# One u tile moved from TensorE to the crossbar, adds of u in another order, and transposes ahead of an output store

## The chip, the cores and the metric

The kernel runs on one core of a Trainium2 chip. The metric is the device time of one execution in microseconds (us), the median over runs. TensorE is PE in the profile, its weight loads PEld, VectorE DVE, ScalarE ACT, GpSimd POOL, SyncE SP.

## The reference

Eight batches of causal attention over a window of 64 positions, then a mixer of low rank along the sequence, then a two layer MLP.

```python
def reference(q, k, v, U, V, w1, w2):        # q, k, v: (8, 8, 576, 64)
    scores = where(0 <= i - j < 64, q @ k.T / 8, -1e9)
    x = concat_heads(softmax(scores) @ v)                # (8, 576, 512)
    u = x + ((x.T @ U) @ V).T                            # rank 32
    return u + relu(u @ w1) @ w2                         # 512 -> 2048 -> 512
```

## The kernel before

The 4608 rows of u are cut into nine chunks of 512 for the MLP. The attention of the next batch is woven into the fills of PE of the current chunk: `slots` lists what follows each fill, and `PLACE` tables give the places. Fills 0 to 15 are the first layer (`ch1`, tile psA), 16 to 31 the second (`ch2`, tile psU, four quarters for each of four row tiles). A batch has 576 rows, four and a half tiles of 128, so chunks and batches do not line up.

The parts that the change touches:

```python
def VM(ts, banks=None):              # u = x + low rank part, for tiles ts
    def up():
        if banks is None:
            pair = ps_big.tile([P, 2, CH], FP32, name="psv", tag="big")
            ...
        for n in range(2):
            nc.tensor.matmul(ps[0][n], vrep[half, ...], hh["sb"][half, ...], ...)
    def add(n):
        def f():
            ...
            nc.vector.tensor_tensor(out=u_tiles[g][rs, cs], in0=ps[0][n][rs],
                                    in1=x[...], op=ALU.add)
        return f
    return [up, add(0), add(1)]

def UT(t):                           # u tile -> its transpose, for the first MLP layer
    def f():
        g = g0 + t
        dst = uT_of(g // TPC)[:, g % TPC, :, :]
        if b >= NXT:                 # NXT = 3: crossbar transpose, issued by SyncE
            nc.sync.dma_start_transpose(out=dst, in_=u_tiles[g][:])
            return
        tp = ps_tp.tile([P, NDC, P], BF16, name="tpu", tag="tp")   # a single bank
        for dc in range(NDC):
            nc.tensor.transpose(tp[:, dc, :], u_tiles[g][...], ident[:])
        nc.scalar.copy(out=dst, in_=tp[:])
    return f

def two_banks():                     # for tile 4: one bank of mm, and the tp bank
    return (psum["mm"].tile(..., name="psv0", tag="mm"),
            ps_tp.tile([P, CH], FP32, name="psv1", tag="tp"))

def mixed(parts=None):
    parts = parts or [VM((NT - 1,), two_banks), VM((0, 1)), VM((2, 3))]
    for part in parts:
        part[0]()
    for part in parts:
        for add in part[1:]:
            add()
```

In the profile, un is a tile of u, psv what the six matmuls of the V part write, uTc the transposed u, and tpu the PSUM tile of a PE transpose; it and psv1 share the one bank of the tag tp, the tp bank. A crossbar transpose is done by the DMA (DMA_TRANSPOSE in the profile). Before the V part, `hh["sb"]` (the low rank result) is spread over the partitions by DVE copies:

```python
nc.scalar.copy(out=part[:], in_=hh["ps"][high])
nc.vector.tensor_tensor(out=hh["sb"][low], in0=hh["ps"][low], in1=part[:], op=ALU.add)
nc.vector.tensor_copy(out=hh["sb"][high], in_=hh["sb"][low])
```

The softmax here doesn't subtract the row's maximum and nothing guards it: scores larger than these inputs give would overflow.

## Time and profile before

| | before |
|---|---|
| median of the first three runs (range) | 311.64 us (311.27 to 311.76) |
| profiled span | 310.6 us |
| PE busy | 301.8 us, 97% |
| first psA matmul | 22.66 us |
| PE transposes into tpu / crossbar transposes into uTc | 36 / 23 |

The first psA matmul divides the span in two: a start-up, in which PE waits for the first loads, and what I call the body, from there to the end of the last add into osb (307.85 us, so 285.19 us). In the body PE hardly stops, so its length is close to a sum of PE pieces. It divides into nine chunks, each from its first psA piece to the next one's in the view of the chain.

### The profile page before, as it was taken

The page shows a single profiled execution, that of the slowest core. Times are in us where ns is not written, and L with a number is a line of the kernel's source. Part 1 is how long each engine was busy: PE and PEld are TensorE (multiplying, and loading weights), DVE is VectorE, ACT ScalarE, POOL GpSimd, SP SyncE. Part 2 cuts the span into 40 slices and gives each one's busy share as a digit, 9 for nine tenths or more (in the row PEclk, how much of TensorE's full clock was granted, in tenths as well). Part 3 has the DMA queues.
Part 4 walks back from the last instruction along what each step waited for, and adds up shares of the span by engine and source line. Part 5 has one row for each costly group of instructions (what it writes and reads, how often), then busy time and mean ns, then how long its engine had stood idle before and what let it go on. Part 6 is the DMA issues. An engine that isn't in the chain of part 4 may idle for free.

```text
span 310.6 us, 6952 instructions
## 1 busy us (share of the span) xinstructions
PE 301.8 (97%) x2881; PEld 147.6 (48%) x2903; DVE 175.1 (56%) x336; ACT 108.2 (35%) x173; POOL 102.0 (33%) x136
## 2 busy tenths in 40 slices
PE   7799999999999999999999999999999999999996
PEld 7453554544545544454445444544454444444443
DVE  4485566528667873677557765666566542116011
ACT  3555680358127620543044304440354004101500
POOL 8693264294695091437143705000000000000000
PEclk9999999999999999999999999999999999999999
DMA  7999999999999999999599999932400275011011
GB/s 107 170 209 208 204 172 145 147 148 160 138 148 157 139 142 203 130 156 172 103 150 141 184 118 132 175 103 74 132 2 0 68 222 203 32 69 36 0 65 70
DMA packets 156495, 39.87 MB, mean 128 GB/s; under 512 B 145040, under 2 KB 151440, under 8 KB 156464
## 3 DMA queue, kind: packets, MB, share of 16 engines
q0 software_dynamic: 104720, 18.88, 82.0%
q1 hardware_dynamic: 51744, 20.55, 34.0%
q8 instruction: 22, 0.36, 0.5%
q14 instruction: 9, 0.07, 0.1%
HBM read 37.97 MB, written 9.44 MB: 153 GB/s over the span
## 4 chain that ended last, share of the span: by engine, by line
PE 93%; DMA 3%; issue 1%; DVE 1%; POOL 1%; ACT 0%; POOLq 0%
PE psA L765 41%; PE psU L789 40%; DMA qr<-in_q_dram 3%; PE sc L347 3%; PE xw L409 2%; PE psv L660 2%; PE pshh L533 1%; PE tpu L694 1%; PE tpg L283 1%; PE low L347 0%; PE psh L533 0%; DVE xs L420 0%; POOL kr L120 0%; PE tpw L283 0%; PE xe L409 0%
## 5 line engine op out<-in xcount | busy, mean ns | idle before, releaser
L765 PE MATMUL psA<-uTc,w1b 128*128 128x512 bf16 (+1 forms) x584 | 131.2, 377 | 0.3 <-DVE uTc L635 0.3
L789 PE MATMUL psU<-w2b,c 128*128 128x512 bf16 (+2 forms) x572 | 127.3, 373 | 1.3 <-issue 0.3
L789 PEld LDWEIGHTS <-c 128*128 128x128 bf16 x592 | 56.0, 98 | 66.0 <-issue 2.9
L765 PEld LDWEIGHTS <-w1b 128*128 128x128 bf16 x584 | 54.3, 98 | 63.9 <-issue 2.6
L777 ACT ACTIVATE c<-psA 128x512 bf16<-128x512 f32 x84 | 50.1, 597 | 83.6 <-PE psA L765 83.3
L775 DVE TENSOR_SCALAR c<-psA 128x512 bf16<-128x512 f32 x60 | 41.3, 689 | 40.9 <-PE psA L765 40.9
L802 DVE TENSOR_TENSOR osb<-psU,un 128x512 f32<-128x512 f32 (+2 forms) x29 | 19.5, 671 | 52.4 <-PE psU L789 52.4
L367 ACT ACTIVATE pts<-sc 128x1024 bf16<-128x1024 f32 x32 | 31.3, 1028 | 2.3 <-PE sc L347 2.3
L138 POOL DMA_DIRECT2D vA<-in_v_dram x32 | 28.3, 913 | 7.4 <-DMA w1b<-in_moe_w_ch_dram 2.7
L675 DVE TENSOR_TENSOR un<-psv,xs 128x512 bf16<-128x512 f32 (+3 forms) x48 | 26.1, 593 | 4.3 <-PE psv L660 4.0
L129 POOL DMA_DIRECT2D qr<-in_q_dram x30 | 26.7, 888 | 4.1 <-PE tpg L283 1.7
L129 POOL DMA_DIRECT2D kr<-in_k_dram x30 | 26.6, 887 | 3.4 <-PE sc L347 2.0
L400 ACT ACTIVATE ptl<-low 128x256 bf16<-128x256 f32 x6 | 2.3, 384 | 61.0 <-PE high L347 61.0
L373 DVE TENSOR_TENSOR pts<-pts,maskA 128x1024 bf16<-128x1024 bf16 x28 | 19.1, 682 | 1.7 <-ACT pts L367 1.7
L500 DVE TENSOR_TENSOR xs<-xw,rcw 128x896 bf16<-128x896 f32 x14 | 15.3, 1091 | 0.5
L963 POOL COPY held<-qf 1x1 bf16<-1x1 bf16 x5 | 0.9, 178 | 42.9 <-DMA qf<-qr 42.9
L347 PEld LDWEIGHTS <-kf 64*64 64x64 bf16 x704 | 9.8, 107 | 7.3 <-issue 7.0
L347 PE MATMUL sc<-qf,kf 64*64 64x128 bf16 (+1 forms) x608 | 11.5, 212 | 0.5 <-DVE qf L300 0.3
L409 PEld LDWEIGHTS <-pts 128*64 128x64 bf16 x512 | 9.8, 110 | 3.5 <-issue 2.5
L697 ACT COPY uTc<-tpu 128x512 bf16<-128x512 bf16 x9 | 5.3, 586 | 11.4 <-PE tpu L694 11.4
L409 PE MATMUL xw<-vA,pts 128*64 128x65 bf16 x217 | 8.4, 195 | 0.0
L974 POOL COPY held<-uTc 1x1 bf16<-1x1 bf16 x3 | 0.5, 177 | 23.6 <-DMA uTc<-un 23.6
(125 smaller groups left out, 190.7 us busy)
## 6 DMA issues: line engine op xcount, KB each, us to landing
out_dram<-osb SPq DMA_DIRECT2D x27, 256.0 KB, 2.3
vA<-in_v_dram POOLq DMA_DIRECT2D x32, 128.0 KB, 6.4
kr<-in_k_dram POOLq DMA_DIRECT2D x24, 128.0 KB, 5.4
qr<-in_q_dram POOLq DMA_DIRECT2D x24, 128.0 KB, 5.5
w2b<-in_moe_w_ch_dram POOLq DMA_DIRECT2D x4, 512.0 KB, 15.8
out_dram<-late SPq DMA_DIRECT2D x8, 256.0 KB, 4.2
vB<-in_v_dram POOLq DMA_DIRECT2D x8, 128.0 KB, 8.8
w1b<-in_moe_w_ch_dram POOLq DMA_DIRECT2D x2, 512.0 KB, 11.1
```

The source lines that it names most:

```text
L129: nc.gpsimd.dma_start(out=dst[0:rows, t, :, :], in_=src[b, :, t * P : t * P + rows, :].rearrange("h p d -> p h d"),)
L138: nc.gpsimd.dma_start(out=dst[:, :, 0:D], in_=v[b, :, lo : lo + P, :].rearrange("h p d -> p h d"))
L347: nc.tensor.matmul(sc[g][r0 : r0 + W, col * W : (col + n) * W], keys_of(j, u, rs), queries_of(j, blk, n, rs), start=not spare, stop=last o ...
L367: nc.scalar.activation(out=dst, in_=sc[:], func=ACT.Exp, scale=scale)
L373: nc.vector.tensor_tensor(out=dst, in0=dst, in1=maskA.rearrange("p g n w -> p g (n w)"), op=ALU.mult)
L409: nc.tensor.matmul(dst, pts[:, h // 2, h % 2, blk, :] if blk < NB - 1 else ptl[:, h // 2, h % 2, :], rhs, start=True, stop=True,)
L675: nc.vector.tensor_tensor(out=u_tiles[g][rs, cs], in0=ps[0][n][rs], in1=x[rs, t, :, :].rearrange("p h d -> p (h d)")[:, cs], op=ALU.add,)
L765: nc.tensor.matmul(ps[i][:, ts.start * P : ts.stop * P], w1b[:, dc, i * P : (i + 1) * P], uTc[:, ts, dc, :], start=(dc == 0), stop=(dc == ...
L775: nc.vector.tensor_relu(out=c1[i][:], in_=ps[i][:])
L777: nc.scalar.activation(out=c1[i][:], in_=ps[i][:], func=ACT.Relu)
L789: nc.tensor.matmul(acc[t][:, lo:hi], c1[i][:, t * P : (t + 1) * P], w2b[:, i, lo:hi], start=(i == 0), stop=(i == NFC - 1),)
L802: nc.vector.tensor_tensor(out=osb[:, lo:hi], in0=acc[t][:, lo:hi], in1=u_tiles[g][:, lo:hi], op=ALU.add,)
```

## The change

One tile (the last of batch 1, the first of chunk 2) goes through the crossbar while SyncE has nothing to do. In the V part of batches 2 to 7, the tiles that are needed first are computed and added first. From batch 3 on, the transposes of u are issued ahead of the output store of the same stretch.

```diff
+    XUT = ((1, 4),)
@@ UT
-                if b >= NXT:
+                if b >= NXT or (b, t) in XUT:
@@ mixed
-                parts = parts or [VM((NT - 1,), two_banks), VM((0, 1)), VM((2, 3))]
+                parts = parts or [VM((0, 1)), VM((2, 3)), VM((NT - 1,), two_banks)]
@@ PLACE
-        "UT": [19, 19, 20, 20, 21],
+        "UT": [18, 18, 19, 19, 20],
@@ PLACE_3
-    PLACE_3 = {**PLACE, "SV": [5, 5, 6, 6], "V": [16], "UT": [17, 17, 18, 18, 19]}
+    PLACE_3 = {**PLACE, "SV": [5, 5, 6, 6], "V": [16], "UT": [16, 16, 16, 18, 18]}
```

## The prediction

> **What bounds the kernel now.** I read the page's first, second and fourth parts, then the waits of the tensor engine (PE), then the chain that ended last in order of time, and last the timelines of SyncE (SP) and of the vector engine (DVE) around the places that the change touches. The page of the kernel before:
>
> ```profile
> span 310.6 us, 6952 instructions
> PE 301.8 (97%) x2881; PEld 147.6 (48%) x2903; DVE 175.1 (56%) x336; ACT 108.2 (35%) x173; POOL 102.0 (33%) x136
> ...
> PEclk9999999999999999999999999999999999999999
> ...
> PE 93%; DMA 3%; issue 1%; DVE 1%; POOL 1%; ACT 0%; POOLq 0%
> ```
>
> PE is busy in 97% of the span, its granted clock is full in all 40 slices, and 93% of the chain that ended last is PE work. The 3% of DMA is the first load of q and k, before the first matmul of real work; the change does not touch it. A busy PE alone need not be a bound, so the second view is what PE itself waited for. The largest rows are of the start, before the first 25 us are over; issue gaps (two of psU, 0.3 us together) are waits for nothing that the profile shows:
>
> ```profile
> PE tpg L283 <- DMA qr<-in_q_dram: 1.6, 1, 1.6
> PE unread L870 <- DVE idle L156: 1.3, 1, 1.3
> PE psU L789 <- issue: 0.3, 2, 0.2
> PE psA L765 <- DVE uTc L635: 0.3, 1, 0.3
> ```
>
> There is no row in which PE waits for a crossbar transpose into uTc, for a copy into uTc from a PE transpose, for an output store, or for the adds of u. So the things that the change moves earlier (transposes ahead of the store, first tiles of u added first) are not what PE waits for now. Only what takes instructions off PE, or puts a new wait on it, can move the time.
>
> **What the Trainium skill says.** "TensorE: Matmul & The Clock Gate", section "Part 4: PE-mode transpose", says that a PE transpose is a matmul against the identity, that its output lands in PSUM and needs a copy after it, and measures about 390 ns for one alone and about 275 ns in one kernel. The trace has 36 of them, at 219 ns each, but these overlap: four in a row cost the chain 0.22 us, 55 ns each. I use the chain's figure, since the chain is what ends. The same page, "Why this matters for your kernels", says that matmuls with few rows that lie in different row groups run concurrently. The trace agrees: six psv matmuls on 32 rows, four of 512 and two of 256 columns, take 0.43 us of the chain where nothing holds them, and a single 512 column matmul takes 0.216 us, so one after the other they would take some 1.1 us. "DMA: Bandwidth & Descriptors", section "Rules for kernel authors", says that transposes from two queues have to be kept apart and that a transpose next to ordinary DMAs needs nothing. All crossbar transposes here are issued by SP, before and after, so the one more needs no new ordering; no run yet shows more than that.
>
> **Part 1: batch 1's last u tile by the crossbar.** It removes four PE transposes and one ACT copy of 586 ns (mean of the copy row), and adds one crossbar transpose on SP. The chain in order of time, columns start, length, piece:
>
> ```profile
> 60.34 0.65 PE psA L765 x4
> ...
> 61.01 2.11 PE psA L765 x12
> 63.12 0.22 PE tpu L694 x4
> 63.34 2.81 PE psA L765 x13
> ```
>
> The piece at 63.12 is the one removed: the third fill of chunk 1 follows the second without a gap, so its 0.22 us come off a chain that has no other work in that place. The ACT copy follows from 63.71 to 64.29 beside matmuls; ACT is idle 65% of the span and PE waits for none of it, so that part is worth 0. The new transpose goes into SP's queue after the ten transposes of batch 2 and before those of batch 3:
>
> ```profile
> 61.16 1.22 SPq L306 DMA_TRANSPOSE qf<-qr  x1
> 70.03 1.19 SPq L306 DMA_TRANSPOSE kf<-kr  x1
> ```
>
> SP is free from 62.38 to 70.03, 7.65 us, held by the load of k. The issue of one uTc transpose takes 1.26 us (median), and it lands 2.5 us later at the median, 6.5 at the worst. The tile's adds end by 61.19, so it issues at about 62.4 and has landed by 69 at the latest. It belongs to chunk 2, whose first matmul is at 93.71: some 24 us to spare. Batch 3's transposes start where they did. Part 1: -0.22 us.
>
> **Part 2: the order of the V part.** For batches 2 to 7 the two full pairs (ps_big) now come first and the half width tile 4 (one bank of mm and the tp bank) last, and so do the adds on DVE. No instruction is added or removed. What PE spends in these six matmuls, for batches 2, 4, 5, 6 and 7:
>
> ```profile
> 86.59 0.93 PE psv L660 x6
> ...
> 145.45 0.70 PE psv L660 x6
> ...
> 177.28 0.50 PE psv L660 x6
> ...
> 208.91 0.43 PE psv L660 x6
> ...
> 240.47 0.43 PE psv L660 x6
> ```
>
> Batch 3's is 0.81. Against 0.43 the 32 row form waits 0.27 us in batch 4 and 0.07 in batch 5. For the 64 row form of batches 2 and 3 I estimate 0.65 us undisturbed (two 512 column pairs and one 256 column pair at 0.216, 0.216 and 0.11, and the same 0.1 of overhead as in the 32 row form, 0.43 less 0.33), so 0.28 and 0.16 are waits. All of these are waits for the copies that spread the low rank result (hh), which stay as they are; whichever psv matmul is first, the row group that comes last has the same columns to do after its copy. I put this at 0, with 0.1 either way.
>
> There is one place where the order can cost. In chunk 1, batch 2's tiles are still transposed on PE, into the same single tp bank that tile 4's second half uses. That half is now added last. DVE and PE there:
>
> ```profile
> 86.84 3.14 DVE L675 TENSOR_TENSOR un<-psv,xs 64x256 bf16<-64x256 f32 x6
> 89.91 0.67 DVE L802 TENSOR_TENSOR late<-psU,un 128x512 f32<-128x512 f32 x1
> ...
> 90.06 0.39 PE L694 MATMUL tpu<-ident,un 128*128 128x128 bf16 x4
> ```
>
> Before, the bank came free after two adds of 0.41 us each (the shortest of the psv adds), at about 87.7. Now it comes free after all six, at about 89.98, and later by 0.1 because the first add waits for a matmul of 512 columns in place of 256. PE comes at 90.06, so a wait of 0 to 0.15 us appears. The instruction order of the changed kernel confirms it: the first of those transposes now waits for DVE where it waited for PE. I put +0.05 us for it.
>
> **Part 3: transposes ahead of the store.** From batch 3 on, SP now issues two to five u transposes and then the store. In chunk 2 the fifth of them and two stores change place, in chunk 3 SP had been held at 137.70 by a store for 12.14 us, and transposes that issued at 149.89 can go at about 147. That makes the next chunk's uTc land some 3 us earlier (first needed at 157.49), and it lets POOL's held copies, which waited 23.6 us for uTc in three places, start the loads of v earlier. PE waits for none of these now, so the worth is 0. The stores move back by at most five issues, about 6.5 us; the output tiles have four buffers and one is filled every 3.5 us or so in this stage, and no more than 0.1 us of wait comes of that.
>
> **Sum.** -0.22 + 0 + 0.05 + 0 = -0.17 us of 311.64, so 311.47; I write 311.4, as the spread of the three runs, 0.49 us, is larger than this last digit.
>
> **Rivals.** (a) The new order turns into a wait: the tp bank is handed over late, or the store that is now behind the transposes holds an output buffer and so PE's psU bank. For it: the handover above is within 0.1 us of PE's arrival. Against it: the four transposes that follow share that bank one after another in any case, and only the first is delayed. It would make 311.7 to 312.2. (b) The earlier transposes and v loads meet other transfers and delay the transposes of q and k that the next chunk's scores need. For it: the DMA engines are 90% busy and more in most slices up to 200 us. Against it: the q and k transposes run a chunk ahead, and the amount moved does not change. It would make 312 to 313. (c) The waits on u are worth more than the trace shows, since the executions that were timed took 1 us longer than the profiled span, and the reorder brings 0.5 to 1 us: 310.7 to 311.1. Against it: no such wait in the chain. (d) The time is PE's alone and only the four transposes count: 311.4. I hold (d) for by far the likeliest.
>
> **Range and chances.** 2% would be 6.2 us. All the gaps of PE after 25 us that the trace could hide, issue (1% of the chain, some 3 us) and the psv waits (0.8 us), are under 4 us together, so the change cannot win 2%; to lose it, one of six chunks would have to stall by 1 us each, which needs (b) on a scale that nothing shows. Faster 0.005, same 0.985, slower 0.01. The range takes the spread of the runs to both sides and half of (a) and (c): 310.9 to 311.9.
>
> **What would show it.** In the changed kernel the PE transposes into tpu should be 32, not 36, ACT copies 8, not 9, crossbar transposes into uTc 24, not 23; the chain should have no piece tpu within chunk 1's third fill, and the first matmul of chunk 2 should come 0.1 to 0.25 us earlier than 93.71. The new transpose should issue near 62.4, and batch 3's should still start near 70. The u transposes of batches 4 to 7 should issue 2 to 3 us earlier and end no PE wait. The psv pieces should stay within 0.1 us of those above. I would be wrong if PE shows a wait for uTc, for osb's store or for un of more than 0.3 us, or if the span from chunk 2's first matmul to the end changes by more than 0.3 us.

## The result and the profile after

The changed kernel took 311.28 us in the median of four runs (311.04 to 311.83), before 311.67 in four runs beside them (311.27 to 311.76). The ratio is 0.9992, interval 0.9975 to 1.001: the same. A ratio here is the mean time of one kernel's fast runs over that of the other's of the same rounds, so it is not quite the ratio of the medians: these differ by 0.39 us, the means by 0.23.

The page after, the lines that answer to those of before:

```profile
span 309.8 us, 6974 instructions
...
PE 303.2 (98%) x2899; PEld 147.8 (48%) x2899; DVE 174.9 (56%) x336; ACT 107.7 (35%) x172; POOL 102.0 (33%) x136
...
PE 93%; DVE 3%; DMA 2%; ACT 1%; issue 1%; POOLq 0%
```

The span is 0.8 us shorter and PE is still 93% of the chain. (PE's count of instructions rises although four were removed: some matmul records of before are missing from its trace.) Two things in the last line are worth a look: DMA has less of the chain, DVE more.

**DMA has less, in the start-up.** The first transposes of q's second half, timeline of PE, before and then after; the bracket is idle time before the row and what ended it:

```profile
12.79 0.45 PE L283 MATMUL tpg<-ident,qr 96*64 96x96 bf16 x12 [1.57 <-DMA qr<-in_q_dram]
```

```profile
11.42 0.45 PE L284 MATMUL tpg<-ident,qr 96*64 96x96 bf16 x12
```

Before, PE waited 1.57 us for that load; after, it did not. The first psA came at 21.87 us in place of 22.66, so 0.79 of the 0.8 us are gained before any changed instruction runs. The bodies are 285.19 and 285.14 us: nothing to tell.

**The tile moved to the crossbar** is gone from PE's chain. In chunk 1 the fills now run through, in the chain in order of time (start, length, piece):

```profile
60.22 8.15 PE psA L766 x40
```

There were 12 matmuls, a tpu piece of 0.22 us and 28 matmuls. The group of PE transposes has 32 left, and it shows what DVE's larger share is:

```profile
L695 PE MATMUL tpu<-ident,un 128*128 128x128 bf16 x32 | 3.1, 219 | 0.2 <-DVE un L676 0.2
```

The last field is idle time of PE before this group, and who ended it: one wait of 0.2 us for the adds of u, which before's group does not have. It sits in chunk 1, at batch 2's first PE transpose. The chain there:

```profile
85.58 0.47 PE psv L661 x2
...
86.08 3.15 DVE un L676 x6
...
89.27 0.38 PE tpu L695 x4
89.65 0.86 PE psU L790 x4
```

For 3.15 us the chain does not run over PE at all but over the six adds of u, and the transpose follows them. PE does matmuls meanwhile, but it ends up late.

**SyncE.** The new transpose goes where it was meant to go:

```profile
61.32 1.32 SPq L307 DMA_TRANSPOSE qf<-qr  x1
62.73 1.22 SPq L691 DMA_TRANSPOSE uTc<-un  x1
71.14 1.19 SPq L307 DMA_TRANSPOSE kf<-kr  x1
```

In chunk 3, the transposes of u no longer stand behind the store:

```profile
145.70 2.56 SPq L691 DMA_TRANSPOSE uTc<-un  x2
148.74 0.33 SPq L816 DMA_DIRECT2D out_dram<-osb  x1
```

The first one issued at 149.89 before. In the waits of POOL, its wait for uTc falls from 23.6 to 16.5 us. No row of PE's waits names uTc's DMA, in either kernel.

So one profile of each says: 0.22 us taken off PE, something lost at the handover, and a gain in the start-up that cannot be the change's. Timed runs with a spread of 0.5 us and more cannot weigh terms of 0.2 us. The body and the chunks of a profile can, if they repeat. That is the first question.

### The profile page after: what moved, and what is told of

It reads as the page before. It is cut to its first block, busy times and chain, and to the rows that moved or that the text cites. A ratio compares the mean times of both kernels' runs of the same rounds, so it can differ in the third digit from the quotient of the medians.

```text
span 309.8 us, 6974 instructions
## 1 busy us (share of the span) xinstructions
PE 303.2 (98%) x2899; PEld 147.8 (48%) x2899; DVE 174.9 (56%) x336; ACT 107.7 (35%) x172; POOL 102.0 (33%) x136
## 4 chain that ended last, share of the span: by engine, by line
PE 93%; DVE 3%; DMA 2%; ACT 1%; issue 1%; POOLq 0%
PE psA L766 41%; PE psU L790 39%; PE sc L348 3%; PE xw L410 2%; DMA kr<-in_k_dram 2%; PE psv L661 1%; DVE un L676 1%; PE pshh L534 1%; PE tpg L284 1%; PE tpu L695 1%; ACT pts L368 1%; PE sc L338 1%; PE tpm L284 0%; PE low L348 0%; PE psh L534 0%
## 5 line engine op out<-in xcount | busy, mean ns | idle before, releaser
L790 PE MATMUL psU<-w2b,c 128*128 128x512 bf16 (+2 forms) x592 | 128.9, 374 | 0.0
L803 DVE TENSOR_TENSOR late<-psU,un 128x512 f32<-128x512 f32 x8 | 5.3, 685 | 5.1 <-PE psU L790 5.0
```

The lines of the kernel that those rows point to most:

```text
L790: nc.tensor.matmul(acc[t][:, lo:hi], c1[i][:, t * P : (t + 1) * P], w2b[:, i, lo:hi], start=(i == 0), stop=(i == NFC - 1),)
L803: nc.vector.tensor_tensor(out=osb[:, lo:hi], in0=acc[t][:, lo:hi], in1=u_tiles[g][:, lo:hi], op=ALU.add,)
```

## The experiments

Twelve more runs, of ten different kernels, were made in three jobs, each on a chip of its own; with the first two that makes fourteen profiles. All gave a correct output. Lengths are in us, from the views of the chain and of PE's timeline; chunk 2 and chunk 3 are those that vary, chunks 4 to 8 were equal within 0.07 us in all fourteen profiles, and chunk 0 took 37.67 to 37.69 in twelve and 37.9 in two. "Copy" is the length of the DVE copy of hh in chunk 1. In the last row the chain leaves PE at the start of chunk 2, so that point is PE's timeline start of the first psA, 91.91, plus the 0.16 by which the two views differ there in other profiles. The runs of a single execution took, in us: in the first job before 310.72 and after 310.81; in the second part 3 alone 311.55; in the third after 310.72, old adds 310.95, transposes later 311.15 and the repeated kernel with (2,3) by the crossbar 311.81, beside one execution of before at 310.86. These are too few to compare.

| kernel | first psA | body | chunk 1 | copy | chunk 2 | chunk 3 |
|---|---|---|---|---|---|---|
| before | 22.66 | 285.19 | 33.37 | 0.61 | 31.95 | 31.83 |
| after | 21.87 | 285.14 | 33.36 | 0.48 | 31.86 | 31.95 |
| before, repeated | 21.82 | 284.48 | 33.09 | 0.29 | 31.78 | 31.64 |
| after, repeated | 21.61 | 284.72 | 33.26 | 0.29 | 31.78 | 31.70 |
| after, third time | 21.63 | 284.64 | 33.26 | 0.29 | 31.79 | 31.62 |
| part 1 alone (crossbar) | 21.63 | 284.22 | 32.86 | 0.29 | 31.79 | 31.56 |
| part 2 alone (order) | 21.73 | 284.92 | 33.48 | 0.29 | 31.79 | 31.68 |
| part 3 alone (places) | 21.48 | 284.54 | 33.23 | 0.47 | 31.78 | 31.56 |
| batch 2 in the old order | 21.50 | 284.23 | 32.86 | 0.29 | 31.84 | 31.56 |
| old adds, new matmul order | 21.58 | 284.90 | 32.87 | 0.29 | 32.05 | 31.77 |
| batch 2's transposes later | 21.76 | 284.92 | 32.76 | 0.46 | 32.48 | 31.71 |
| old order, (2,3) by crossbar | 22.05 | 284.40 | 32.64 | 0.29 | 32.06 | 31.73 |
| the same, repeated | 23.46 | 284.05 | 32.64 | 0.29 | 31.79 | 31.66 |
| (2,2) by crossbar too | 21.42 | 284.80 | 32.75 | 0.66 | 32.25 | 31.56 |

### The two kernels again

No edit. Before once more:

> The kernel before once more, unchanged, for the spread. I split each profile at the first psA matmul. The stretch from there to the end of the last add into osb, called the body, was 285.19 us before (22.66 to 307.85) and 285.14 after (21.87 to 307.01); the start-up before it was 0.79 us shorter after, where PE did not wait for the second half of q (1.57 us before, no row after). Theory A (the whole 0.8 us of the profiled span is start-up luck, the body is fixed by PE): this repeat has a body of 285.1 to 285.3, while its start-up may lie anywhere from 21.5 to 23. Theory B (the body also wanders by some tenths of a us, so that nothing of the change's parts can be read from single profiles): the body differs from 285.19 by more than 0.2.

The changed kernel once more, and a third time in the last job:

> The changed kernel once more, unchanged. Theory A: body 285.0 to 285.3 again, and a wait of PE for the un adds at the first of batch 2's PE transposes of 0.2 us again, since it comes of the order of the adds. Theory B: body off by more than 0.2 from 285.14, or no such wait this time. If the shorter start-up belongs to the change, it starts its first psA near 21.9 again while the repeat of before starts near 22.7; if it is luck, the two are in no order.

> The changed kernel a third time, for the spread of chunk 1. My theory: 33.2 to 33.5 us again, with the wait for un of 0.2 us, so the late handover is there in every execution and takes back the 0.22 us that the removed transposes gave. Rival: below 33.0, the wait gone, and the first two were chance.

Theory A half fell. The start-up is luck: first psA matmuls of one and the same kernel lay 0.8 us apart (before: 22.66 and 21.82), and 21.42 to 23.46 over all fourteen, in no order with the edits. But the body of before was 284.48, 0.71 less than in its first profile, so the body wanders too, as B said, and the bodies of the two first profiles told nothing. Chunk 1 of before took 33.37 and 33.09, chunk 2 31.95 and 31.78, chunk 3 31.83 and 31.64.

What wanders can be seen. Chunk 1's six psv matmuls wait for the DVE copy of hh. The timelines of POOL and DVE in before's first profile:

```profile
85.72 0.93 POOL L129 DMA_DIRECT2D qr<-in_q_dram  x1
...
86.15 0.61 DVE L555 COPY hh<-hh 64x512 bf16<-64x512 bf16 x1
```

and in its repeat:

```profile
83.35 2.73 POOL L138 DMA_DIRECT2D vA<-in_v_dram  x3
...
85.31 0.29 DVE L555 COPY hh<-hh 64x512 bf16<-64x512 bf16 x1
```

It is the same copy, 0.61 us long in one and 0.29 in the other. POOL issues DMAs one after another here, one in some 0.87 us. In the repeat the copy starts 0.23 us after an issue began (the last of those three, at 85.08), in the first profile 0.43 us after. Of the fourteen copies, nine took 0.29 us; the five others took 0.46 to 0.66, with the psv matmuls longer by up to 0.34 us. "SBUF — State Buffer", section "Who interferes with whom", says that DVE copies in a two port mode and GpSimd exclude each other from a shared port pair, and that the one who comes second waits for the whole instruction. The trace agrees with the exclusion, but not with the whole instruction: the five long copies started 0.34 to 0.55 us into an issue and ended 1.01 to 1.04 us after it began, while the nine short ones started at 0.03 to 0.23, or at 0.78 and 0.84. The short copies of hh and vB (64 or 32 partitions by 512 or 520) in all fourteen traces after 25 us repeat this: of 116 that start during an issue, the 50 of its first 0.25 us all took 0.27 to 0.29; the 37 that start 0.26 to 0.64 us into it all took longer, 0.33 to 0.80; and the 29 later ones took 0.28 to 0.43. With no issue under way, 150 of 150 took 0.27 to 0.29. So it is the phase to an issue that makes a copy long; that the cause is this lock is an inference, as no run here took POOL away.

So chunk 1 is only to be compared at the same length of the copy. At 0.29: before 33.09; changed, twice, 33.26, both times with the wait for un of 0.2 us. **The change costs chunk 1 0.17 us**, where I had expected to gain 0.17.

### Part 1 alone

```diff
+    XUT = ((1, 4),)
-                if b >= NXT:
+                if b >= NXT or (b, t) in XUT:
```

> Only part 1 of the change: batch 1's last u tile through the crossbar; order of the adds and places as before. My theory: the four transposes are taken off PE's chain and nothing is put in their place, so the body is 0.22 us shorter than before, 284.97 (284.9 to 285.1), with no PE wait for un at the transposes of batch 2. Rival: the tile's crossbar transpose delays batch 3's q and k or something else that PE meets later, and the body stays at 285.1 or above. Time against before: ratio 0.999, not to be told from 1 in three rounds.

Chunk 1 took 32.86 us, 0.23 less than before, with no wait for un. The body was 284.22, below the 284.9 to 285.1 forecast, which was counted from before's first profile; before's repeat had 284.48. Time: 311.03 against 311.28, ratio 0.9981 (0.9958 to 1.0005). My theory holds. One thing did move: batch 3's transposes on SyncE started at 70.7 to 71.14 in the five profiles that I read with the new transpose ahead of them, and at 69.7 to 70.15 in the four without. PE did not wait for them in any.

### Part 2 alone

```diff
-                parts = parts or [VM((NT - 1,), two_banks), VM((0, 1)), VM((2, 3))]
+                parts = parts or [VM((0, 1)), VM((2, 3)), VM((NT - 1,), two_banks)]
```

> Only part 2: the two full pairs first and tile 4 last, in matmuls and adds. My theory after seeing the result: the tp bank is handed over late in chunk 1, so PE waits 0.2 us for un at the first transpose of batch 2, and the body is 0.1 to 0.3 us longer than before: 285.3 to 285.5. Rival (the prediction's 0.05 and noise): body 285.1 to 285.25 and a wait under 0.1. Time against before: ratio 1.0005, not to be told from 1.

Chunk 1 took 33.48 us, 0.39 more than before's 33.09, with the wait for un of 0.2. The body, 284.92, missed the 285.3 to 285.5 expected, again because that was counted from before's first profile; against the repeat's 284.48 it is 0.44 longer. Chunks 2 and 3 were those of before within 0.04. Time: 311.43 against 311.28, ratio 0.9997 (0.9973 to 1.0021). 0.39 less 0.23 is 0.16, and the whole change cost 0.17: the two parts add up. The profile's row says 0.2 us, but PE lost twice that. PE's matmuls overlap and the ends in the profile are modelled, so the idle time in the row is what lies beyond a modelled end; without the wait, the first transpose starts some 0.16 us ahead of that end (in the repeat of before at 88.94 in PE's timeline, against 89.10 in the chain). From the psv piece to the psU piece behind the first transpose, the chain takes 3.57 us in the repeat of before:

```profile
85.76 0.65 PE psv L660 x6
86.41 2.70 PE psU L789 x12
89.10 0.22 PE tpu L694 x4
89.33 0.86 PE psU L789 x4
```

and 3.96 in the third profile of the changed kernel (85.35 to 89.31), 0.39 more:

```profile
85.35 0.37 PE psv L661 x2
...
85.74 3.15 DVE un L676 x6
...
88.93 0.38 PE tpu L695 x4
89.31 0.86 PE psU L790 x4
```

### Part 3 alone

```diff
-        "UT": [19, 19, 20, 20, 21],
+        "UT": [18, 18, 19, 19, 20],
-    PLACE_3 = {... "UT": [17, 17, 18, 18, 19]}
+    PLACE_3 = {... "UT": [16, 16, 16, 18, 18]}
```

> Only part 3: the crossbar transposes of batches 3 to 7 ahead of the output store; all else as before. My theory: PE waits for neither, so the body is that of before less the psv excess: chunk 1 33.09, chunk 2 31.61 to 31.8, chunks 3 to 7 between 31.55 and 31.7, all within 0.1 of the repeat of before. Rival: the earlier transposes bring some tenths of a us at the starts of chunks 3 to 7, or the stores behind them cost as much.

Chunks 3 to 7 took 31.56, 31.55, 31.56, 31.56 and 27.62 us, as in the repeat of before but for chunk 3's 31.64, which has a psv piece 0.09 longer there (0.52 against 0.43). Chunk 1's 33.23 has a copy of 0.47 and a psv piece of 0.79 in place of 0.65: 33.09 without. The places are worth nothing here, in either direction. The single time was 311.55.

### What in the order costs: batch 2 back in the old order

```diff
-                parts = parts or [VM((0, 1)), VM((2, 3)), VM((NT - 1,), two_banks)]
+                parts = parts or (
+                    [VM((NT - 1,), two_banks), VM((0, 1)), VM((2, 3))]
+                    if b == 2
+                    else [VM((0, 1)), VM((2, 3)), VM((NT - 1,), two_banks)]
+                )
```

> The whole change, but batch 2 alone keeps the old order (tile 4 first in matmuls and adds). The length of chunk 1, from its first psA to that of chunk 2, is 33.09 us in the repeat of before, 32.86 with part 1 alone, 33.48 with part 2 alone, 33.26 in the repeat of the changed kernel. My theory: the reorder costs chunk 1 some 0.4 us, because the adds that come last hand over the tp bank late, and only batch 2 has transposes on PE behind them. So chunk 1 takes 32.8 to 33.0 here (up to 0.3 more where the psv matmuls wait for the copies of hh, which I subtract as the excess of the psv piece over 0.65), with no wait for un. Rival: the loss is something else of the reorder, such as the places or SyncE's order, and chunk 1 stays at 33.2 or above. Time against before: ratio 0.998 to 1.0.

Chunk 1 took 32.86 us and PE no longer waits for un: all of the loss is batch 2's, and it is gone. Time: 310.34 against 311.08, ratio 0.9971 (0.9940 to 1.0001).

### Adds or matmuls

The new order of matmuls, with tile 4 added first:

```diff
-                for part in parts:
+                for part in (parts if b < 2 else parts[-1:] + parts[:-1]):
                     for add in part[1:]:
                         add()
```

> The whole change with the new order of the six psv matmuls, but the adds of tile 4 first again, for batches 2 to 7. My theory: the bank is back after the first two adds, so there is no wait for un at the first transpose of batch 2, and chunk 1 takes 32.86 us, at most 0.15 more, as the first add now waits for the last psv matmul and the whole row of adds ends later; psv excess over 0.65 subtracted. Rival: it is the matmul order that costs, and chunk 1 stays at 33.2 to 33.5. Chunks 3 to 7 stay at 31.55 to 31.7 in both.

Chunk 1 took 32.87 us. The chain of the place, in this kernel:

```profile
85.54 0.65 PE psv L661 x6
86.19 1.83 PE psU L790 x8
...
88.88 0.22 PE tpu L695 x4
89.11 0.86 PE psU L790 x4
```

From psv to the psU behind the transpose it is 3.57 us again. The matmul order costs nothing; the order of the adds costs 0.39. (One profile, but it agrees within 0.01 us with part 1 alone and with batch 2 in the old order.) Chunk 2 was longer than expected, 32.05; its chain runs over DVE, and one of the copies into vB (0.28 us in the timeline of before) takes 0.65 there: it starts 0.31 us into a DMA issue of POOL, as the long copies of hh do. I did not expect that; it comes up again below.

### Transposes later

```diff
 PLACE_2
-        "UT": [28, 29, 30, 31],
+        "UT": [29, 30, 31, 102],
```

> The whole change with its new order for every batch, but batch 2's four PE transposes come one place later each (after the second, third and fourth quarter of chunk 1's last tile, and the fourth after the third fill of chunk 2, as before for batch 1). My theory: the order as such costs nothing, only the handover of the tp bank to a transpose that comes too soon does. So no wait for un, and chunks 1 and 2 together take 64.64 us less any psv excess over 0.65 (32.86 and 31.78, as with batch 2 in the old order), while four transposes only move from chunk 1 to chunk 2 (0.22 us). Rival: the new order costs PE by itself (how the six psv matmuls pack), and the two chunks stay at 64.9 or above.

PE does not wait for un, with the new order in place. Chunk 1 took 32.76 with a copy of 0.46 and a psv piece of 0.77: 32.64 without the excess, that is 32.86 less the four transposes that moved to chunk 2. So the bank and not the order is what PE waited for. The sum of the chunks, though, is 65.24, above the forecast by 0.48 after the excess: chunk 2 has the long way over DVE again (a vB copy of 0.67 us, from 0.32 us into an issue), on top of the 0.22 of its new transposes. I leave open whether the transposes there add to it; as a remedy the old order for batch 2 is the better one.

### Further: a second tile by the crossbar

Batch 2's tile 3 is the first of chunk 3, so it has long to land; not a whole chunk, as it turned out, since it was issued only at 109.91 us in the first profile, behind transposes of q and k, with chunk 3 beginning at 124.43. In addition to the old order for batch 2:

```diff
-    XUT = ((1, 4),)
+    XUT = ((1, 4), (2, 3))
```

> As the last, and batch 2's last whole tile (the first of chunk 3, needed 31 us later) is transposed by the crossbar too, so four more transposes leave PE. My theory: another 0.22 us off chunk 1, 32.6 to 32.75 less any psv excess over 0.65, the other chunks unchanged at about 31.6. It should be the fastest of all: 0.45 us below before in the body. Rival: batch 4's q and k transposes, which come right behind it on SyncE, are put back and PE waits for them at the start of chunk 3. Time against before: ratio 0.9985, hardly to be told from 1 in five rounds.

> The candidate for the best kernel once more, unchanged (batch 2 in the old order, its last whole tile by the crossbar). Its chunk 2 took 32.06 us in the first profile, against 31.78 to 31.86 elsewhere. My theory: that was chance, a copy into vB on the vector engine held beside GpSimd's DMA issues, so now chunk 1 takes 32.64 and chunk 2 31.8. Rival: it belongs to this kernel (one more transpose in front of batch 4's q and k), and chunk 2 is above 32.0 again.

Chunk 1 took 32.64 us in both, another 0.22 less. Chunk 2 took 32.06 the first time, with a vB copy of 0.66 us (0.49 us into an issue), and 31.79 the second, with one of 0.28 outside any issue: chance, as the first theory said. PE shows no wait for batch 4's transposes of q and k in either. The body of the repeat, 284.05 us, is the shortest of all, although its span is the second longest: its first psA came at 23.46. Time in five rounds: 310.54 against 311.08, ratio 0.9968 (0.9941 to 0.9996). That is a gain over before, by an interval that just leaves out 1. I do not credit all of it to the edit: the chunks explain 0.45 us (33.09 to 32.64), 0.14%, and the measured 0.32% has the start-ups in it. It also leans on one of before's eleven executions, of 313.5 us at a granted clock of 0.995, where the others took 310.62 to 311.71; without it the ratio of the means would be 0.9975. The 0.9971 above leans on it too.

### And one too many

Batch 2's tile 2 too, which chunk 2 needs in its first fill; adds and places so that the crossbar can start at once:

```diff
-    XUT = ((1, 4), (2, 3))
+    XUT = ((1, 4), (2, 2), (2, 3))
@@ mixed, b == 2
+                    [VM((NT - 1,), two_banks), VM((2, 3)), VM((0, 1))]
 PLACE_2
-        "UT": [28, 29, 30, 31],
+        "UT": [28, 29, 25, 25],
```

> As the last, but batch 2's third tile (the last of chunk 2, needed some 0.7 us into that chunk, only about 5 us after its add) goes through the crossbar as well, with the adds in the order tile 4, 2 and 3, 0 and 1, and the two crossbar issues right after them. My theory: PE saves another 0.22 us, but a crossbar transpose takes 1.2 us to issue and 2.4 to 7.4 us to land, so PE waits for uTc at the start of chunk 2, by 0 to 3 us; I expect about 1 us lost in chunk 2, and a row of PE waiting for the DMA of uTc. Rival: landing takes 2.5 us here and the tile is in time, so chunk 1 falls to 32.4 and no such row shows.

Here the crossbar ends a wait of PE. The chain, and the row of PE's waits:

```profile
86.99 5.99 DMA uTc<-un
...
93.02 0.38 PE psA L770 x4
```

```profile
PE psA L770 <- DMA uTc<-un: 0.3, 1, 0.3
```

The transpose issued at 86.99 and had landed 5.99 us later. Chunk 1 is 0.34 longer by the copy of hh (0.66 us, psv from 0.71 to 1.05 in PE's timeline), so 32.41 without, 0.23 less than with (2,3) alone; chunk 2 took 32.25, some 0.45 more than 31.79. The four transposes saved 0.22 and the late landing cost twice that (both chunks together, which need no point between them: 64.66 without the 0.34, against 64.43). I had expected 1 us. Time: 310.66, ratio 0.9984 (0.9946 to 1.0021), not to be told from the others.

## Why the prediction was right or wrong

The time, 311.28 against 311.4, lies inside the range, and "same" was right for the reason given: nothing in the change reaches 1% of a span that PE fills. The sum behind it was wrong in sign. It said -0.17 us; at equal copies the change costs +0.17. That the measured median fell by 0.39 and came out near 311.4 is luck: the interval of the ratio takes in 1, and in the one pair with profiles all of the gain was in the start-up (the other timed executions have no profile to look at).

- **Part 1 was right**: -0.22 forecast, -0.23 measured. The transpose issued in SyncE's gap and PE waited for nothing of it. Batch 3's transposes did not start where they did, but about 1 us later.
- **Part 2, the order as such, was right** at 0: with the adds put back, the matmul order costs nothing, and chunks 3 to 7 of part 2 alone are those of before.
- **Part 2, the handover, is the step that failed.** The mechanism was named, but its term, "I put +0.05 us for it", was 0.39. The two numbers set against each other, adds ending at 89.98 and PE coming at 90.06, came from a profile in which PE itself had been held at psv by a copy of 0.61 us. That hold put PE back by 0.28 us; the adds, which follow the first psv matmul, were not put back. With a copy of 0.29 us, in the repeat of before, PE comes at 88.94, 0.21 us ahead of the end of the adds at 89.15. In the changed kernel the first add starts 0.14 us later after the first psv matmul (0.46 us, against 0.32), where the prediction took 0.1, and from the last add to the transpose it is 0.05: together 0.40, and 0.39 was measured. I had even put down this psv piece as holding 0.28 us of wait, but did not take it off PE's time of arrival two lines on.
- **The psv waits** were rightly read as waits for the copies of hh, and wrongly taken for something that stays: they come and go with the phase of POOL's issues, and batch 2's 0.93 was 0.65 in the repeat of before. The estimate of 0.65 for an undisturbed piece was exact.
- **Part 3 was right** at 0: transposes 3 us or so earlier, and no wait of PE changes.
- **The rivals.** (a) happened in its first half, a late tp bank, at 0.39 us and not with the stores. (b) did not happen: no run shows a new wait of PE for q or k; the one wait for a crossbar transpose came where I pushed a tile into the last 6 us before its use, and was for that tile itself. (c), hidden gains of 0.5 to 1 us, did not: it is the start-up that moves by so much. (d), PE's transposes alone, held to be by far the likeliest, is part 1's measurement but leaves out the handover; its 311.4 was near the median by luck.
- **The signs to look for.** 32, 8 and 24 were right. The first matmul of chunk 2 was to come 0.1 to 0.25 us earlier; counted from the first psA at equal copies it came 0.17 later, the one sign that would have told. The 0.3 us threshold for a wait on un was not reached by the row (0.2), though it was by the chain (0.39): rows of idle time understate what PE loses. From chunk 2's first matmul to the end it took 213.71 us in the repeat of before and 213.77 in that of the changed kernel, as forecast.

## What to carry to other kernels

When the effects of a change are a few tenths of a us, cut the profile at the points where the bound engine starts each stage, and compare stages between repeats before you compare times; two profiles of before differed by 0.84 us in the start-up and by 0.71 in the body. When you work out a margin between two engines, make sure that neither was held up by something accidental in that very profile. Where two uses share one buffer, look at how soon the second comes, and put the work that frees the buffer first if it comes soon. Give a transpose to the crossbar only where its tile is needed clearly later than the landing (up to 8.2 us here).

## What the Trainium skill lacked or had wrong

- "TensorE: Matmul & The Clock Gate", "Part 4: PE-mode transpose": gives 390 and about 275 ns for a transpose. Here each record is 219 ns, and in a row of four one costs PE's chain 55 ns; removing four saved 0.22 to 0.23 us in three experiments. That section has no figure for transposes in a row, which is the one that decides; the page has figures only for ordinary matmuls of that width back to back.
- "SBUF — State Buffer", "Who interferes with whom": it says that a blocked copy waits for the other's whole instruction. Here an issue of a DMA by POOL, 0.9 us long, held up no DVE copy that started in its first 0.25 us (50 of 50 ran at 0.27 to 0.29 us), and every one that started 0.26 to 0.64 us into it (37 of 37, at 0.33 to 0.80 us). The page does not say in which part of an issue the port is taken.
- "DMA: Bandwidth & Descriptors", "DMA Transpose (X-bar)": has no landing time for a crossbar transpose of one 128 by 512 tile in SBUF. Here it was 2.4 us at the least and 2.5 to 5.8 at the median of a profile, up to 8.2 us beside other transfers, and 5.99 in the one case where PE waited for it.
